# The last 64 tokens of v: 512-byte rows of four heads, with even and odd keys apart

## The chip, the core and the metric

One core of a Trainium2 chip runs the kernel. Its engines each work through their own instructions in order: TensorE (PE in the profile; PEld is its weight load), VectorE (DVE), ScalarE (ACT), GpSimd (POOL) and SyncE (SP), which here only issues transfers. Transfers run on the core's 16 DMA engines; GpSimd issues some too. The metric is the time of one execution on the device in microseconds (us); lower is better. A run of the kernel is profiled, and the profile tells for each instruction when it ran and what it waited for.

## The reference

Attention with 8 heads in a sliding window of 128 keys, then a spectral mixing layer:

```python
# q, k, v: (8, 8, 576, 64)
scores = scale * np.matmul(q, k.transpose(0, 1, 3, 2))
bias = slopes[:, None, None] * (-np.abs(rel))[None]      # rel = query - key
mask = (rel >= 0) & (rel < 128)
scores = np.where(mask, scores + bias[None], -1e9)
attn = softmax(scores)
x = np.matmul(attn, v)                                   # -> (8, 576, 512)
X = np.fft.rfft(x, axis=1)
Y[:, :64] = complex product of X[:, :64] with w_r + i w_i # per mode a 512x512 matrix
u = x + np.fft.irfft(Y, n=576, axis=1)
out = u + np.maximum(u @ w_ch, 0.0)
```

The weights w_r and w_i are 64 matrices of 512x512 each in float32: 134 MB, by far the most that is read.

## The kernel before

**Units.** Attention is cut into 32 units, one for each batch and pair of heads (s is the pair, 0 to 3). `GROUPS = ((0,), (1, 2, 3))`: first the eight batches of pair 0, then for each batch the pairs 1, 2 and 3. When the units of pair 0 are done, the weight rows that belong to these two heads can be used (group 0, 64 loads of 512 KB); the others (group 1, 64 loads of 1536 KB) follow when attention is over.

**Slots.** `_slot` (L589) writes the order out by hand. Slot n holds, in this order, the scores of unit n in two halves (`_score`), the transposes of unit n+1 (`_tr`, `_evac`), GpSimd's casts of q and k of unit n+2 (`_cast_qk`) and of v of unit n+1 (`_cast_v`), the tail of v (below), the spectrum of unit n-2, the product with v of unit n-1 (`_av`), and from slot 10 on some of the weight products of group 0 (`_modes`, L704). Each engine takes its part of this in order.

**Loads.** SP issues q, k (288 KB each), v (two of 128 KB per unit) and the weights, in one order, and ahead of their use: nine units of q and k, six of v. The weights go into a ring of 12288 columns, which holds 12 loads of group 0 or 4 of group 1; `_load_w` (L645) issues a load where its columns have been used. The program's semaphores let a load go only when the eighth load before it has landed.

**Keys on partitions.** For the first 512 tokens a partition holds two neighbouring tokens of v (`"(k p r) d -> p k (r d)"` with r=2, 512 bytes), and the scores are computed with even keys on partitions 0 to 63 and odd keys on 64 to 127 (`kT[hs, c * P + r : c * P + P : 2]`). The mask tile holds exp(-slope * distance) for these positions; it is multiplied to exp(scores) by VectorE. It is made at the start: `_consts` (L243) lays out the distances in `rel` on VectorE, and `_mask` (L308) takes two activations for a pair of heads.

**The tail.** 576 is 4.5 times 128, so 64 tokens are left. Their keys stand in natural order on 64 partitions, a second copy for the second head on the other 64:

- `_load_vt` (L378), on GpSimd's queue, loads for one pair of heads the tail of all eight batches: two transfers of 64 partitions x 8 rows of 256 bytes. `_cast_vt` (L388) casts the 128x512 to bf16 in `vbt`. Both are done once a pair: for pair 0 ahead of slot 0, for the pairs 1 to 3 in the slots 2 to 4 (load) and 4 to 6 (cast).
- in `_score`, four matmuls of 64x64 (L455) write the tail's scores of both heads, to both halves of the partitions.
- in `_av`, two matmuls (L499), one for each head, add the tail's product; L504 and what follows on VectorE divides by the sums.

GpSimd has four kinds of work in the slots, then: casts of q and k (L397), of v (L409), of the tail (L389), and the issue of the tail's transfers (L382).

Of the kernel before, what the change touches and what calls it, by code (L numbers as in the profile page):

```python
# [9 lines left out]
FP32 = mybir.dt.float32  # L10
BF16 = mybir.dt.bfloat16
I32 = mybir.dt.int32
AF = mybir.ActivationFunctionType
# [3 lines left out]
P = 128  # L17
MB = 8
GROUPS = ((0,), (1, 2, 3))
# [25 lines left out]
def kernel(  # L45
# [52 lines left out]
    with tc.manual_schedule(engines={ET.SP, ET.PE, ET.Activation, ET.DVE, ET.Pool}):  # L98
        with ExitStack() as wctx:
# [5 lines left out]
            with ExitStack() as actx:  # L105
                cp = actx.enter_context(tc.tile_pool(name="const", bufs=1))
# [5 lines left out]
                g.vbs = [cp.tile([P, 8, 72], BF16, name=f"vb{i}") for i in range(3)]  # L112
                g.vbt = cp.tile([P, NP, B, 72], BF16)
                g.qpool = actx.enter_context(tc.tile_pool(name="qk", bufs=QK))
                g.vpool = actx.enter_context(tc.tile_pool(name="v", bufs=VB))
                g.vts = actx.enter_context(tc.tile_pool(name="vts", bufs=2))
                g.work = actx.enter_context(tc.tile_pool(name="work", bufs=2))
# [17 lines left out]
                with tc.tile_pool(name="tmpc", bufs=1, side="right") as tp:  # L135
                    _consts(g, tp)
                    _cast_qk(g, 0)
                    for s in GROUPS[0]:
                        _load_vt(g, s)
                    _cast_qk(g, 1)  # L140
                    _cast_v(g, 0)
                    for s in GROUPS[0]:
                        _cast_vt(g, s)
                    _tr(g, 0, 0)
# [27 lines left out]
                for n in range(3, N + 2 + TAIL):  # L172
# [6 lines left out]
                    h = (len(w) + 1) // 2  # L179
# [63 lines left out]
def _consts(g, tp):  # L243
    nc = g.nc
# [6 lines left out]
    nc.gpsimd.iota(reli, [[1, 256]], base=0, channel_multiplier=-2)  # L251
    rel3i = tp.tile([P, 64], I32)
    nc.gpsimd.iota(rel3i, [[1, 64]], base=0, channel_multiplier=-1)
    make_identity(nc, g.ident_b)
    nc.gpsimd.tensor_tensor(
        out=g.ident2, in0=g.ident_b[:, 0:64], in1=g.ident_b[:, 64:128], op=ALU.add)
    for vb in g.vbs:
        nc.gpsimd.memset(vb[:, :, g.D : g.D + 1], 1.0)
    nc.gpsimd.memset(g.vbt[:, :, :, g.D : g.D + 1], 1.0)

# [30 lines left out]
    FAR = float(2**15)  # L291
    rel = tp.tile([P, 512], FP32)
    g.rel = rel
    nc.vector.tensor_copy(rel[:, 0:256], reli)
    nc.vector.tensor_scalar_add(rel[64:128, 0:256], rel[64:128, 0:256], 127.0)
    nc.vector.tensor_copy(rel[:, 448:512], rel3i)
    nc.vector.tensor_scalar_add(rel[64:128, 448:512], rel[64:128, 448:512], 64.0)
    off = tp.tile([P, 256], FP32)
    for r in (rel[:, 448:512], rel[:, 0:256]):
        o = off[:, : r.shape[1]]  # L300
        nc.vector.tensor_scalar(o, r, 0.0, FAR, op0=ALU.is_lt, op1=ALU.mult)
        nc.vector.tensor_tensor(out=r, in0=r, in1=o, op=ALU.max)
    nc.vector.tensor_scalar(off, rel[:, 0:256], float(P), FAR, op0=ALU.is_ge, op1=ALU.mult)
    nc.vector.tensor_tensor(out=rel[:, 0:256], in0=rel[:, 0:256], in1=off, op=ALU.max)
# [3 lines left out]
def _mask(g, tp, s):  # L308

    for hh in range(2):  # L310
        g.nc.scalar.activation(  # L311
            g.mask[:, s, hh], g.rel, AF.Exp, scale=-(2.0 ** (-8.0 * (2 * s + hh + 1) / g.H)))

# [63 lines left out]

def _load_vt(g, s):  # L378

    vt = g.vts.tile([P, g.B, g.D], FP32, tag="vt", name=f"vt{s}")  # L380
    for hh in range(2):
        g.nc.gpsimd.dma_start(  # L382
            out=vt[64 * hh : 64 * hh + 64],
            in_=g.v[:, 2 * s + hh, 512:576, :].rearrange("b p d -> p b d"))
    g.unit["vt", s] = vt


def _cast_vt(g, s):  # L388
    g.nc.gpsimd.tensor_copy(g.vbt[:, s, :, 0 : g.D], g.unit.pop(("vt", s)))  # L389

# [42 lines left out]
def _score(g, n, w):  # L433
# [7 lines left out]
    for i in range(2):  # L441
        c = 2 * w + i
        nq = 256 if c < 3 else 192
        for r in range(2):
            for hh in range(2):
# [4 lines left out]
                    start=True, stop=True, tile_position=(64 * hh, 64 * r))  # L450
    if w:
        for r in range(2):
            for hh in range(2):
                hs = slice(64 * hh, 64 * hh + 64)
                nc.tensor.matmul(  # L455
                    sc[64 * r : 64 * r + 64, hh, 448:512], lhsT=kT[hs, 512:576],
                    rhs=qT[hs, 512:576], start=True, stop=True, tile_position=(64 * hh, 64 * r))
    a = g.work.tile([P, 2, 512], BF16, tag=f"att{w}", name=f"att{w}")
# [13 lines left out]
def _av(g, n):  # L472
# [10 lines left out]
    def col(t):  # L483
        return slice(t * (D + 1), (t + 1) * (D + 1))

    for t in range(ST):
# [3 lines left out]
        for hh in range(2):  # L490
            for j, (c, q0) in enumerate(terms):
# [4 lines left out]
                    start=(j == 0), stop=(t < 4 and j == len(terms) - 1), **kw)  # L496
    for hh in range(2):
        hs = slice(64 * hh, 64 * hh + 64)
        nc.tensor.matmul(  # L499
            av[ps, hh, col(4)], lhsT=att[1][hs, hh, 448:512], rhs=g.vbt[hs, s, b, 0 : D + 1],  # L500
            start=False, stop=True, tile_position=(64 * hh, po))
    avv = av[:, :, 0 : ST * (D + 1)].rearrange("p h (t c) -> p h t c", t=ST)
# [86 lines left out]
def _slot(g, n, w0, w1):  # L589
# [21 lines left out]
    if n + 1 < N:  # L611
        _cast_v(g, n + 1)
    for j, grp in enumerate(GROUPS[1:]):
        for i, s in enumerate(grp):
            if n == g.first[j + 1] - 4 + i:
                _cast_vt(g, s)
        for i, s in enumerate(grp):
            if n == g.first[j + 1] - 6 + i:
                _load_vt(g, s)
    if 0 <= n - 2 < N - 1:  # L620
# [299 lines left out]
```

## Time and profile before

| | |
|---|---|
| time, median of 3 runs (lowest to highest) | 448.21 us (445.66 to 448.3) |
| the profiled execution | 450.29 us; its span 448.5 us |
| TensorE, VectorE, ScalarE, GpSimd busy | 66%, 48%, 42%, 31% of the span |
| read from HBM, written | 163.58 MB, 9.44 MB |
| transfers issued by GpSimd (the tail of v) | 8 of 128 KB, 7.5 us to landing (median) |
| loads of weights | 1536 KB: 13.8 us to landing; 512 KB: 7.4 to 8.0 |
| chain of waits, by engine | DMA 50%, TensorE 26%, ScalarE 10%, VectorE 6% |

The span has three parts. Up to 166 us attention runs, with group 0's weight products from slot 10 on. From there to about 402 us TensorE takes group 1's weights as they land. Then comes the finish, with the last products and the output. Lines of the profile name an engine, the line of the kernel, the operation, `out<-in`, and, in a timeline, what ended the idle time before it in brackets. "x16" is a number of instructions merged into one line. In the view by stretches there are for each stretch its length, the busy time of each engine with its number of instructions, TensorE's granted clock (1 is full), the share of the 16 DMA engines' time that packets took, and GB/s.

### The profile page before, as it was taken

How to read it: one execution, taken by the hardware profiler on the slowest of the kernel's cores; microseconds unless marked ns; L12 is line 12 of the kernel's file. 1: busy time of each engine (PE TensorE's matmuls, PEld its weight loads, DVE VectorE, ACT ScalarE, POOL GpSimd, SP SyncE). 2: the span in 40 equal slices, each digit the busy share in tenths (PEclk: the TensorE clock that was granted, in tenths of full speed). 3: DMA queues.
4: the chain of work that ended last, by engine and by line, in shares of the span. 5: the costliest groups of instructions: out<-in, count | busy, mean ns of one | idle time of the engine just before them, and what ended most of it. 6: DMA issues, size and time to landing. Idle time of an engine off the chain costs nothing.

```text
span 448.5 us, 12893 instructions
## 1 busy us (share of the span) xinstructions
PE 294.1 (66%) x5506; PEld 204.2 (46%) x5527; DVE 216.1 (48%) x427; ACT 189.6 (42%) x302; POOL 139.1 (31%) x257
## 2 busy tenths in 40 slices
PE   2467989887787885222235664854856748696993
PEld 2455767666666763111123333432433334464661
DVE  8458566566765661010002543453535345462882
ACT  3787656584866741000011331322313233251794
POOL 7699889586876702020000000000000000000700
PEclk9969576686988975555555988589778587899997
DMA  8999999999999999999999999999999999996498
GB/s 249 346 335 327 388 325 353 347 390 379 392 368 375 393 415 429 432 425 426 430 427 433 426 429 429 427 430 426 430 429 430 426 429 430 427 428 282 185 374 288
DMA packets 51562, 173.86 MB, mean 388 GB/s; under 512 B 4912, under 2 KB 21296, under 8 KB 43440
## 3 DMA queue, kind: packets, MB, share of 16 engines
q1 hardware_dynamic: 51120, 171.99, 97.2%
q0 software_dynamic: 384, 1.05, 0.9%
q8 instruction: 43, 0.70, 0.6%
q14 instruction: 15, 0.12, 0.1%
HBM read 163.58 MB, written 9.44 MB: 386 GB/s over the span
## 4 chain that ended last, share of the span: by engine, by line
DMA 50%; PE 26%; ACT 10%; DVE 6%; issue 4%; POOL 2%; ACTq 0%; POOLq 0%
DMA ring<-in_moe_w_r_dram 47%; ACT att L459 6%; PE acc L704 5%; PE sc L447 4%; PE xt L539 4%; PE u L825 3%; PE av L493 3%; DMA ring<-in_moe_w_i_dram 3%; ACT qkT L428 3%; PE tqk L420 2%; PE u L745 2%; POOL qkb L397 1%; PE xw L758 1%; DVE x_sb L507 1%; ACT mask L311 1%
## 5 line engine op out<-in xcount | busy, mean ns | idle before, releaser
L704 PE MATMUL acc<-Xz,ring 128*128 128x32 bf16 x2048 | 70.7, 183 | 100.2 <-DMA ring<-in_moe_w_r_dram 51.0
L704 PEld LDWEIGHTS <-ring 128*128 128x128 bf16 x2048 | 61.3, 101 | 130.1 <-DMA ring<-in_moe_w_r_dram 65.1
L763 ACT CAST hl<-xw 64x512 bf16<-64x512 f32 x72 | 41.7, 579 | 105.6 <-PE xw L758 70.9
L459 ACT ACTIVATE att<-sc 128x1024 bf16<-128x1024 f32 x64 | 65.6, 1025 | 32.8 <-PE sc L447 26.7
L764 DVE TENSOR_TENSOR hl<-xw,hl 64x512 bf16<-64x512 f32 x72 | 49.6, 688 | 58.1 <-ACT hl L763 57.8
L409 POOL CAST vb<-v 64x256 bf16<-64x256 f32 x128 | 64.7, 505 | 20.1 <-PE av L493 13.7
L783 POOL MEMSET ZTa<- 32x512 bf16 x2 | 1.0, 515 | 187.5 <-ACT ZTa L781 187.5
L447 PE MATMUL sc<-qkT,qkT 64*64 64x256 bf16 (+1 forms) x512 | 32.4, 330 | 30.1 <-ACT qkT L428 16.3
L758 PE MATMUL xw<-wch,xT 128*128 128x512 bf16 x138 | 46.3, 467 | 2.7 <-issue 2.2
L428 ACT COPY qkT<-tqk 128x576 bf16<-128x576 bf16 x64 | 40.7, 638 | 0.6 <-PE tqk L420 0.6
L420 PE MATMUL tqk<-ident_b,qkb 64*64 64x64 bf16 x1152 | 31.7, 214 | 7.6 <-POOL qkb L397 6.9
L420 PEld LDWEIGHTS <-qkb 64*64 64x64 bf16 x1152 | 30.8, 130 | 10.2 <-POOL qkb L397 9.2
L464 DVE TENSOR_TENSOR att<-att,mask 128x1024 bf16<-128x1024 bf16 x32 | 26.9, 839 | 14.7 <-ACT att L459 14.5
L585 ACT ACTIVATE Xz<-xz 128x192 bf16<-128x192 f32 (+1 forms) x24 | 7.5, 313 | 59.0 <-DVE Xz L584 57.9
L493 PE MATMUL av<-vb,att 128*128 128x65 bf16 (+1 forms) x512 | 30.8, 215 | 0.6 <-issue 0.2
L584 DVE CAST Xz<-xz 128x384 bf16<-128x384 f32 (+1 forms) x24 | 12.0, 511 | 36.4 <-PE xz L578 35.7
L447 PEld LDWEIGHTS <-qkT 64*64 64x64 bf16 x512 | 13.1, 120 | 35.3 <-ACT qkT L428 18.8
L397 POOL CAST qkb<-k 128x576 bf16<-128x576 f32 x32 | 27.5, 859 | 0.0
L493 PEld LDWEIGHTS <-att 128*128 128x128 bf16 (+1 forms) x512 | 24.4, 111 | 6.5 <-issue 0.6
L397 POOL CAST qkb<-q 128x576 bf16<-128x576 f32 x32 | 24.6, 768 | 6.1 <-PE tqk L420 3.3
L738 DVE COPY xT<-tp 128x512 bf16<-128x512 bf16 x36 | 15.2, 421 | 21.9 <-PE tp L736 21.4
L469 DVE TENSOR_TENSOR att<-att,mask 128x1024 bf16<-128x1024 bf16 x32 | 25.0, 780 | 1.5 <-ACT att L459 1.1
(104 smaller groups left out, 395.2 us busy)
## 6 DMA issues: line engine op xcount, KB each, us to landing
ring<-in_moe_w_r_dram SPq DMA_DIRECT2D x32, 1536.0 KB, 13.8
ring<-in_moe_w_i_dram SPq DMA_DIRECT2D x31, 1536.0 KB, 13.7
ring<-in_moe_w_i_dram SPq DMA_DIRECT2D x33, 512.0 KB, 8.0
ring<-in_moe_w_r_dram SPq DMA_DIRECT2D x32, 512.0 KB, 7.4
q<-in_q_dram SPq DMA_DIRECT2D x32, 288.0 KB, 6.3
k<-in_k_dram SPq DMA_DIRECT2D x32, 288.0 KB, 6.2
v<-in_v_dram SPq DMA_DIRECT2D x64, 128.0 KB, 5.8
out_dram<-o SPq DMA_DIRECT2D x32, 256.0 KB, 3.3
```

The lines of the kernel that those rows point to most:

```text
L397: g.nc.gpsimd.tensor_copy(tb, t)
L409: g.nc.gpsimd.tensor_copy(o[64 * r : 64 * r + 64, i], v[64 * i : 64 * i + 64, r])
L420: g.nc.tensor.transpose(tp[hs, r, :], u.b[w][hs, r], g.ident_b[hs, hs], tile_position=(64 * hh, 64 * hh))
L428: g.nc.scalar.copy(dst.rearrange("c (p r) -> c p r", r=g.R), u.tp[w].rearrange("c r p -> c p r"))
L447: nc.tensor.matmul(sc[64 * r : 64 * r + 64, hh, 256 * i : 256 * i + nq], lhsT=kT[hs, c * P + r : c * P + P : 2], rhs=qT[hs, c * P : c * P ...
L459: nc.scalar.activation(a, sc, AF.Exp, scale=1.0 / math.sqrt(g.D))
L464: nc.vector.tensor_tensor(out=a, in0=a, in1=m, op=ALU.mult)
L493: nc.tensor.matmul(av[o, hh, col(t)], lhsT=att[c // 2][:, hh, q0 : q0 + m], rhs=u.vb[:, 2 * c + hh, 0 : D + 1], start=(j == 0), stop=(t < ...
L704: nc.tensor.matmul(acc[:, et, :, m0 - c0 : m0 - c0 + n, :], lhsT=wt[:, a, et * P : (et + 1) * P], rhs=X[:, a, 1 - w : 3 - w, m0 % MB : m0 ...
L758: nc.tensor.matmul(xw, lhsT=xT[:, dt], rhs=g.wch[:, dt], start=(dt == 0 and n in RELU), stop=(dt == 3))
L763: nc.scalar.copy(g.hl[own, n, h], xw[own])
L764: nc.vector.tensor_tensor(out=g.hl[other, n, h], in0=xw[own], in1=g.hl[own, n, h], op=ALU.subtract)
```

## The change

The tail of v is loaded by batch and not by pair of heads. A partition now holds two neighbouring tokens (512 bytes) of one head, four heads fill 128 partitions, and two transfers load the eight heads of a batch. So the even and the odd keys of a head stand on the same 32 partitions, one behind the other, and the tail's scores must be laid out the same way: those of head hh of pair s on 32 partitions, with even keys in the first bank of the scores and odd keys in the second, where each bank belonged to one head before.

```diff
-                g.vbt = cp.tile([P, NP, B, 72], BF16)
+                g.vbt = cp.tile([P, B, 2, 2, 72], BF16)
...
-                g.vts = actx.enter_context(tc.tile_pool(name="vts", bufs=2))
+                g.vts = actx.enter_context(tc.tile_pool(name="vts", bufs=4))
...
-                    for s in GROUPS[0]:
-                        _load_vt(g, s)
+                    for b in range(2):
+                        _load_vt(g, b)
                     _cast_qk(g, 1)
                     _cast_v(g, 0)
-                    for s in GROUPS[0]:
-                        _cast_vt(g, s)
...
-    nc.vector.tensor_copy(rel[:, 448:512], rel3i)
-    nc.vector.tensor_scalar_add(rel[64:128, 448:512], rel[64:128, 448:512], 64.0)
+    nc.vector.tensor_copy(rel3, rel3i.rearrange("p r q -> p (r q)"))
+    for i in range(1, 4):
+        nc.vector.tensor_scalar_add(rel3[32 * i : 32 * i + 32], rel3[32 * i : 32 * i + 32], 64.0 * i)
...
+    for i in (1, 3):
+        nc.vector.tensor_scalar_mul(rel3[32 * i : 32 * i + 32], rel3[32 * i : 32 * i + 32], 0.5)
...
     for hh in range(2):
         g.nc.scalar.activation(
-            g.mask[:, s, hh], g.rel, AF.Exp, scale=-(2.0 ** (-8.0 * (2 * s + hh + 1) / g.H)))
+            g.mask[:, s, hh, 0:448], g.rel, AF.Exp,
+            scale=-(2.0 ** (-8.0 * (2 * s + hh + 1) / g.H)))
+    g.nc.scalar.activation(
+        g.mask[:, s, :, 448:512], g.rel3.rearrange("p (r q) -> p r q", r=2), AF.Exp,
+        scale=-(2.0 ** (-8.0 * (2 * s + 1) / g.H)))
...
-def _load_vt(g, s):
-
-    vt = g.vts.tile([P, g.B, g.D], FP32, tag="vt", name=f"vt{s}")
-    for hh in range(2):
+def _load_vt(g, b):
+
+    vt = g.vts.tile([P, 2, 2, g.D], FP32, tag="vt", name=f"vt{b}")
+    for i in range(2):
         g.nc.gpsimd.dma_start(
-            out=vt[64 * hh : 64 * hh + 64],
-            in_=g.v[:, 2 * s + hh, 512:576, :].rearrange("b p d -> p b d"))
-    g.unit["vt", s] = vt
-
-
-def _cast_vt(g, s):
-    g.nc.gpsimd.tensor_copy(g.vbt[:, s, :, 0 : g.D], g.unit.pop(("vt", s)))
+            out=vt[:, i].rearrange("p r d -> p (r d)"),
+            in_=g.v[b, 4 * i : 4 * i + 4, 512:576].rearrange("h (p r) d -> h p (r d)", r=2))
+    g.unit["vt", b] = vt
+
+
+def _cast_vt(g, b):
+    g.nc.gpsimd.tensor_copy(g.vbt[:, b, :, :, 0 : g.D], g.unit.pop(("vt", b)))
...
     if w:
+        a = 64 * (1 - s % 2)
         for r in range(2):
-            for hh in range(2):
-                hs = slice(64 * hh, 64 * hh + 64)
-                nc.tensor.matmul(
-                    sc[64 * r : 64 * r + 64, hh, 448:512], lhsT=kT[hs, 512:576],
-                    rhs=qT[hs, 512:576], start=True, stop=True, tile_position=(64 * hh, 64 * r))
+            hs = slice(64 * r, 64 * r + 64)
+            nc.tensor.matmul(
+                sc[a : a + 64, r, 448:512], lhsT=kT[hs, 512:576], rhs=qT[hs, 512:576],
+                start=True, stop=True, tile_position=(64 * r, a))
+        for hh, r in ((0, 0), (1, 1), (1, 0), (0, 1)):
+            hs = slice(64 * hh, 64 * hh + 64)
+            a = 64 * (s % 2) + 32 * hh
+            nc.tensor.matmul(
+                sc[a : a + 32, r, 448:512], lhsT=kT[hs, 512 + r : 576 : 2],
+                rhs=qT[hs, 512:576], start=True, stop=True, tile_position=(64 * hh, a))
...
-    for hh in range(2):
-        hs = slice(64 * hh, 64 * hh + 64)
-        nc.tensor.matmul(
-            av[ps, hh, col(4)], lhsT=att[1][hs, hh, 448:512], rhs=g.vbt[hs, s, b, 0 : D + 1],
-            start=False, stop=True, tile_position=(64 * hh, po))
+    for r in range(2):
+        for hh in range(2):
+            a = 64 * (s % 2) + 32 * hh
+            nc.tensor.matmul(
+                av[ps, hh, col(4)], lhsT=att[1][a : a + 32, r, 448:512],
+                rhs=g.vbt[a : a + 32, b, s // 2, r, 0 : D + 1],
+                start=False, stop=(r == 1), tile_position=(a, po))
...
-    for j, grp in enumerate(GROUPS[1:]):
-        for i, s in enumerate(grp):
-            if n == g.first[j + 1] - 4 + i:
-                _cast_vt(g, s)
-        for i, s in enumerate(grp):
-            if n == g.first[j + 1] - 6 + i:
-                _load_vt(g, s)
+    if n < g.B:
+        _cast_vt(g, n)
+    if n + 2 < g.B:
+        _load_vt(g, n + 2)
```

A pair of heads uses 64 of the 128 partitions of the tail's scores (which half depends on s). The first two matmuls in `_score` fill the other half with scores that nothing reads, so that the activation over the whole tile reads defined values. Per unit the tail has six matmuls in the scores where it had four, and four in the product with v where it had two. The tail's loads and casts lie in the slots 0 to 7: in slot n the cast of batch n, and behind it the load of batch n+2; the batches 0 and 1 are loaded ahead of slot 0.

More of the change, by code (lines that the diff above doesn't have):

```diff
@@ L251, in _consts @@
     nc.gpsimd.iota(reli, [[1, 256]], base=0, channel_multiplier=-2)
-    rel3i = tp.tile([P, 64], I32)
-    nc.gpsimd.iota(rel3i, [[1, 64]], base=0, channel_multiplier=-1)
+    rel3i = tp.tile([P, 2, 64], I32)
+    nc.gpsimd.iota(rel3i, [[-1, 2], [1, 64]], base=0, channel_multiplier=-2)
     make_identity(nc, g.ident_b)
@@ L258, in _consts @@
         nc.gpsimd.memset(vb[:, :, g.D : g.D + 1], 1.0)
-    nc.gpsimd.memset(g.vbt[:, :, :, g.D : g.D + 1], 1.0)
+    nc.gpsimd.memset(g.vbt[:, :, :, :, g.D : g.D + 1], 1.0)
     pcol = tp.tile([P, 1], FP32)
@@ L291, in _consts @@
     FAR = float(2**15)
-    rel = tp.tile([P, 512], FP32)
-    g.rel = rel
+    rel = tp.tile([P, 448], FP32)
+    rel3 = tp.tile([P, 128], FP32)
+    g.rel, g.rel3 = rel, rel3
     nc.vector.tensor_copy(rel[:, 0:256], reli)
     nc.vector.tensor_scalar_add(rel[64:128, 0:256], rel[64:128, 0:256], 127.0)
-    nc.vector.tensor_copy(rel[:, 448:512], rel3i)
-    nc.vector.tensor_scalar_add(rel[64:128, 448:512], rel[64:128, 448:512], 64.0)
+    nc.vector.tensor_copy(rel3, rel3i.rearrange("p r q -> p (r q)"))
+    for i in range(1, 4):
+        nc.vector.tensor_scalar_add(rel3[32 * i : 32 * i + 32], rel3[32 * i : 32 * i + 32], 64.0 * i)
     off = tp.tile([P, 256], FP32)
-    for r in (rel[:, 448:512], rel[:, 0:256]):
+    for r in (rel3, rel[:, 0:256]):
         o = off[:, : r.shape[1]]
```

## The prediction

> **What bounds the kernel now.** I began with busy time in stretches of the span, cut where GpSimd's queue q0 is busy in the DMA view (it carries vt alone).
>
> ```profile
> core 0: us, PE busy (x) PEld busy (x) DVE busy (x) ACT busy (x) POOL busy (x), PEclk, DMA share, GB/s
> ...
> 9.00:13.30 4.30, 0.78 (x30) 0.69 (x25) 2.72 (x8) 1.73 (x4) 0.93 (x3) 1.00 1.09 241
> 13.30:29.10 15.80, 8.88 (x225) 7.15 (x224) 8.68 (x20) 13.89 (x21) 14.04 (x23) 0.92 1.05 378
> 29.10:33.40 4.30, 4.12 (x81) 3.38 (x79) 2.32 (x6) 3.12 (x5) 4.13 (x8) 0.50 1.08 244
> ...
> 35.50:38.70 3.20, 2.49 (x55) 1.52 (x47) 3.10 (x7) 2.75 (x4) 2.80 (x6) 1.00 1.03 286
> ...
> 41.20:44.90 3.70, 1.80 (x52) 1.20 (x50) 3.03 (x6) 2.43 (x4) 3.55 (x7) 0.84 1.04 302
> 44.90:60.00 15.10, 13.48 (x291) 10.41 (x286) 8.96 (x21) 9.61 (x14) 12.35 (x22) 0.70 1.06 377
> ```
>
> The DMA share is at or above 1.0 in every stretch, and stays at 1.01 with 428 GB/s from 166 to 405 us. No compute engine's share comes near that. But the rate differs: 378 GB/s in the loads of q, k, v and weights, 241 to 302 while the four pairs of vt transfers move. SP's timeline agrees that the DMA stream bounds: nearly every load from 58 to 166 us is issued within 0.1 us of the landing of the eighth load before it. So compute matters only if it lets that stream run dry. The chain of waits shows how far that is:
>
> ```profile
> 164.98 0.82 PE av L493 x9
> 165.80 0.20 PE av L499 x2
> 165.99 0.36 PE acc L704 x10
> 166.35 11.95 DMA ring<-in_moe_w_r_dram
> 178.30 0.05 issue
> 178.35 0.84 PE acc L704 x24
> 179.20 13.68 DMA ring<-in_moe_w_r_dram
> ```
>
> Up to 166 us the chain runs through compute, behind it through weights. The load issued at 166.35 waited for ring rows that attention's last weight products free. It lands 11.95 us later. Its 1.573 MB need 3.7 us at 428 GB/s, and a transfer has some 2.7 us of fixed time (3.3 us to landing for 256 KB of output, less 0.6 for the bytes). The other 5.6 us it stood behind older loads. That is the cover: compute of the first stage can end 5.6 us later before the end moves, and each microsecond by which the stream gets shorter takes one off the cover. So the end moves by the larger of two numbers: the change S of the stream, and (delay D of compute at 166 us) - 5.6.
>
> **The stream, S.** Removed: 8 transfers of 128 KB in 256-byte rows, 8 x 64 x 8 = 4096 rows. Added: 16 of 64 KB in 512-byte rows, 2048 rows, the same 1.05 MB. In the four stretches with vt 4.12 MB moved in 15.5 us (sum of rate times length). The 3.07 MB that are not vt would need 8.1 us at 378 GB/s, so vt costs the stream 7.4 us, 29 ns a row on each of 16 engines. The nearest row for the new form is v itself: in the trace's packet records a 512-byte row of v holds its engine for 28 ns. So a row costs the same at 256 and at 512 bytes, and half the rows cost 3.7 us: a gain of 3.7. Bounds: vt at the plain rate of 378 GB/s would cost 2.8 us (gain 4.6); if the cost goes with bytes, the gain is nothing. Eight more transfers bring 128 more semaphore packets of 17 ns, 0.1 us. SP's own queue keeps its order. I take S = -3.6, between -4.5 and +0.1.
>
> The Trainium skill (DMA: Bandwidth & Descriptors, "Why small descriptors are slow") speaks against that: a fixed 3 cycles on top of one per 32 bytes, so 11 cycles for 256 bytes and 19 for 512. By it the new rows cost 7.4 x 19/22 = 6.4 us, and S would be an estimated -1.0; the equal 28 and 29 ns above speak for the price by rows.
>
> **Compute, D.** *GpSimd.* Each vt DMA takes it 0.68 us to issue.
>
> ```profile
> 5.56 1.52 POOL L382 DMA_DIRECT2D vt<-in_v_dram  x2
> 7.08 0.68 POOL L397 CAST qkb<-q 128x576 bf16<-128x576 f32 x1
> ...
> 14.50 0.75 POOL L389 CAST vbt<-vt 128x512 bf16<-128x512 f32 x1 [4.48 <-DMA vt<-in_v_dram]
> ```
>
> Before: 8 issues (5.5 us), 4 casts of 0.61 (2.5) and the 4.5 us in which it stands at 10 to 14.5 us, 12.5 in all. After: 16 issues (10.9) and 8 casts of half the size (0.3 to 0.4 each by proportion, 2.7), 13.6, without the wait: the first cast now stands behind the casts of units 2 and v of unit 1, some 4 us of work. It adds 2.7 us before the casts of unit 1, then 1.7 us in each of slots 0 to 5. That engine is on the chain from 30 to 45 us, where the casts of q, k, v queue behind the issues and TensorE's transposes wait for them. Laid out slot by slot with the rows' durations (q, k 1.2; v 2.1 to 2.6) it reaches the casts of units 6 to 10 between 0.3 and 1.7 us sooner than before. A vt cast comes some 9 us behind its issue, landing took 7.5: if landing takes 2 us more, each of six slots stalls up to 1 us. Taken as 0, between -1 and +4.
>
> *Start.* Vector work for the tail's mask grows from 4 small operations to 8, at 0.3 to 0.44 us from one start to the next (L295 to L302): 1.2 to 1.8 us ahead of ScalarE's first mask, and each head pair's mask grows by one activation, some 0.2. ScalarE's first exp moves from 13.05 to about 14.8 us. In 15 to 30 us the chain is ScalarE, but from 30 us it is GpSimd, whose place is no later; the transposes waited up to 4.8 us for it. I cost this at 0, and at 2 if GpSimd's cover is gone.
>
> *TensorE.* Per unit two more matmuls in the tail's scores and two in its av, and tiles of 64x32 and 32x64.
>
> ```profile
> 152.59 0.39 PE L447 MATMUL sc<-qkT,qkT 64*64 64x256 bf16 x8
> 152.81 0.20 PE L455 MATMUL sc<-qkT,qkT 64*64 64x64 bf16 x4
> 152.94 0.78 PE L493 MATMUL av<-vb,att 128*128 128x65 bf16 x16
> 153.65 0.22 PE L499 MATMUL av<-vbt,att 64*64 64x65 bf16 x2
> 153.80 0.57 PE L704 MATMUL acc<-Xz,ring 128*128 128x32 bf16 x16
> ```
>
> Four tail scores on four tiles run side by side, and the next group starts 0.13 us behind them, 0.15 behind the two of L499, where matmuls of one shape follow at 0.03 to 0.05. So going from one tile shape to another costs about 0.13. The Trainium skill (TensorEngine Tiling, "Key Properties") has it that a change of tiling mode drains the array; these rows agree. New per unit: one more change of shape (64x64 to 64x32), 0.13, and a second wave on the same tiles in each tail, 0.03 to 0.08 each: 0.19 to 0.29 us. At the lower clock of 60 to 80 us (0.66) the same step reads 0.20 (64.37 to 64.57), so 0.3 in the mean. The first eight units are GpSimd's; over the other 24 it is 7.2 us, and TensorE holds 57% of the chain in 60 to 80 us: 4.1. Bounds: 2.6 (0.19 x 24 x 0.57) and 14 (0.43 x 32, all on the chain). DVE's reciprocal waits for the longer tail; that is in the same sum.
>
> D = 4.1, from 1.6 to 14. Then D - 5.6 = -1.5 against S = -3.6: the end moves by -1.5. The stage behind 166 us and the finish are untouched. The profiled execution took 450.29 us (span 448.5 and 1.8 around it), 2.1 above the median of 448.21; on its own time the sum gives 448.8, on the median's 446.7.
>
> **The rivals.** 1. *Rows cost by bytes.* S lies between -1 and 0, compute is covered anyway: 447.2 to 448.3. For it: the slow stretches also hold v's rows. Against: 29 ns a row.
>
> 2. *Compute outruns its cover* (slower). The tail's changes of shape cost at the upper bound, or GpSimd stalls on vt. It decides from D = 5.6 on, microsecond for microsecond: D = 8 gives 450.6, 0.43 x 32 = 13.8 gives 456.4. For it: GpSimd is busy 94% in 60 to 80 us and TensorE 85%, so little absorbs a delay. Against: the 57%.
>
> 3. *Too few engines carry vt* (slower). The source's outer dimension is now four heads. If a transfer ran on the same four engines each time, these would hold 4 packets of 4 KB at 252 ns (the packet records' mean for q0) for each of 16 transfers, 16 us instead of 4, and every load is spread over all: +12, 460. If the four change from transfer to transfer, the load is even and nothing is lost but some microsecond of landing. The Trainium skill (DMA: Bandwidth & Descriptors, "Why a DMA increments its semaphore by 16 and not by 1") says that the outer dimension limits the engines, and that GpSimd's transfers take turns over the 16; no run here shows either yet.
>
> 4. *All of S arrives* (D at most 2, S to -4.5): 443.7 to 444.7.
>
> **How the numbers follow.** Likeliest case (-3 to 0 net, 445.2 to 448.2) 0.45; rival 1 0.2; rival 2 0.2, half of it over 452.7; rival 3 0.05; rival 4 0.1. A measurement of this kernel can tell about 1%, 4.5 us, from no change: below 443.7 lies the far end of rival 4 (0.07), above 452.7 half of rival 2 and rival 3 (0.15), between them 0.78. The range leaves out rival 3, the upper part of rival 2 and the far end of rival 4: 443.2 to 452.6.
>
> **What would show it.** Right: the dips to 241 to 302 GB/s around vt become shallower or half as long; GpSimd has no wait of 4.5 us for vt; the first load of 1536 KB is issued some 4 us later than 166.35 and still stands behind older loads. Wrong: the dips keep their area (S), TensorE's last av lies 6 us or more later (D), or vt's landing goes well past 8 us.

## The result: slower by 1.2%, and the profile after

The changed kernel takes 453.8 us (median of 6 runs, 451.8 to 455.28); the kernel before took 448.05 on the same chip (6 runs, 445.52 to 451.23). The ratio is 1.0121, 95% interval [1.0089, 1.0153]: 5.4 us more, between 4.0 and 6.9. The forecast was 446.7, and its chance of slower by over 1% was 0.15. The profiled execution of the changed kernel took 451.8 (span 450.0), the lowest of its six, while the one of the kernel before (450.29) lay 2.2 above its median. So both kernels were profiled once more: **e7** is the kernel before (447.47, span 445.7), **f4** the changed one (452.63, span 450.9).

First the stretches in which the tail of v moved before, now of the changed kernel (columns as in the prediction):

```profile
core 0: us, PE busy (x) PEld busy (x) DVE busy (x) ACT busy (x) POOL busy (x), PEclk, DMA share, GB/s
9.00:13.30 4.30, 1.30 (x36) 1.16 (x37) 4.05 (x9) 0.37 (x1) 4.11 (x9) 1.00 1.12 261
13.30:29.10 15.80, 8.46 (x219) 6.73 (x219) 7.94 (x18) 13.21 (x23) 15.22 (x28) 0.98 1.08 340
29.10:33.40 4.30, 2.71 (x37) 1.94 (x38) 1.49 (x5) 3.62 (x6) 4.11 (x8) 0.50 1.06 333
...
41.20:44.90 3.70, 3.14 (x85) 2.46 (x84) 2.96 (x8) 2.90 (x5) 3.59 (x6) 0.87 1.06 316
44.90:60.00 15.10, 11.73 (x322) 9.36 (x321) 11.42 (x26) 10.86 (x14) 13.40 (x23) 1.00 1.06 359
```

The dips are shallower (261, 333 and 316 GB/s where 241, 244 and 302 stood), but what lay between them has fallen too: 340 for 378, 359 for 377. The dip is spread out, not smaller. GpSimd's timeline shows the wait gone, as was forecast; a cast of the tail finds its data there and follows its neighbours without a bracket:

```profile
14.87 0.40 POOL L395 CAST vbt<-vt 128x256 bf16<-128x256 f32 x1
15.21 1.35 POOL L388 DMA_DIRECT2D vt<-in_v_dram  x2
```

Now the chain of waits of the changed kernel at the end of attention:

```profile
169.18 0.81 PE av L505 x9
169.99 0.25 PE av L512 x3
170.24 0.36 PE acc L715 x10
170.60 7.94 DMA ring<-in_moe_w_r_dram
178.54 0.05 issue
178.59 0.82 PE acc L715 x24
179.41 0.02 issue
179.43 14.43 DMA ring<-in_moe_w_r_dram
```

The first load of 1536 KB is issued at 170.60 and not at 166.35: 4.25 us later, nearly the 4.1 that was forecast. But it lands only 7.94 us after its issue where that was 11.95. Of the 5.6 us that it stood behind older loads, 1.6 are left. The older loads were not there, and why shows in what SP waited for from 140 to 170 us (in total, times, longest), first in e7, then in the changed kernel:

```profile
SPq L661 <- DMA ring<-in_moe_w_r_dram: 5.7, 8, 1.0
SPq L661 <- PE acc L704: 5.4, 8, 2.6
```

```profile
SPq L672 <- PE acc L715: 15.0, 8, 3.4
SPq L672 <- DMA ring<-in_moe_w_i_dram: 1.4, 2, 0.7
```

In the changed kernel SP no longer waits for a landing but for TensorE, whose weight products free the ring's columns: 15.0 us (15.1 in f4), against 5.4 in e7 and 1.5 in the first profile of before. That wait alone is no loss yet, though. In e6 (the kernel before with sixteen transfers of the tail, see below), which takes as long as the kernel before, SP waits as long for TensorE from 140 to 170 us, and by the chain of waits its first large load is issued late too and lands as soon after that:

```profile
SPq L662 <- PE acc L705: 14.2, 9, 2.6
```

```profile
167.54 7.96 DMA ring<-in_moe_w_r_dram
```

What counts is whether the stream keeps its rate. That is read from four stretches of the span; two of them for the changed kernel, e7, e3 (the kernel before with the new loads alone) and, the second only, e6:

```profile
0.00:60.00 60.00, 36.82 (x884) 28.89 (x885) 40.67 (x97) 39.84 (x57) 55.36 (x104) 0.89 1.03 324
...
160.00:180.00 20.00, 15.99 (x302) 11.75 (x302) 9.51 (x24) 6.83 (x11) 2.46 (x16) 0.76 0.92 342
```

```profile
0.00:60.00 60.00, 39.20 (x886) 30.48 (x887) 40.62 (x94) 41.77 (x57) 50.28 (x94) 0.87 1.02 331
...
160.00:180.00 20.00, 10.60 (x183) 7.45 (x180) 5.21 (x15) 2.11 (x5) 2.44 (x16) 0.51 1.03 426
```

```profile
0.00:60.00 60.00, 39.23 (x846) 31.03 (x847) 40.88 (x93) 39.57 (x53) 53.16 (x103) 0.89 1.03 317
...
160.00:180.00 20.00, 12.04 (x235) 8.64 (x233) 8.26 (x22) 4.16 (x7) 2.46 (x16) 0.67 1.03 425
```

```profile
160.00:180.00 20.00, 12.90 (x252) 9.52 (x252) 8.82 (x23) 4.69 (x8) 2.44 (x16) 0.62 1.02 417
```

From 180 to 400 us all run at 428 GB/s. Between 160 and 180 us the changed kernel moves 342 GB/s where e7 moves 426: 84 x 20 us = 1.68 MB less, 3.9 us of the stream at 428. Its span is 4.3 longer. That is where the time goes, as against e7. The first profile of before moves 424 GB/s in this stretch, but had moved less ahead of it, 371 GB/s from 60 to 160 us where the changed kernel moved 385 and e7 381:

```profile
60.00:160.00 100.00, 83.21 (x2007) 67.88 (x2004) 63.04 (x136) 67.03 (x94) 74.56 (x126) 0.80 1.03 371
...
160.00:180.00 20.00, 12.52 (x223) 8.90 (x220) 8.03 (x21) 4.15 (x7) 2.44 (x16) 0.58 1.03 424
```

So the two executions that were profiled first lie only 1.5 us apart. Up to 180 us e7 has moved 66.5 MB, the first profile of before 65.4, the changed kernel 64.8 and f4 64.9. The new loads alone do not dent this stretch (425); they slow the first 60 us instead, 317 for 331, 0.84 MB or 2.0 us.

### The profile page after: what moved, and what is told of

Read it like the earlier page. It is cut to its first block, busy times and chain, and to the rows that moved or that the text cites. A ratio compares the mean times of both kernels' runs of the same rounds, so it can differ in the third digit from the quotient of the medians.

```text
span 450.0 us, 13172 instructions
## 1 busy us (share of the span) xinstructions
PE 297.0 (66%) x5634; PEld 207.2 (46%) x5655; DVE 218.2 (48%) x431; ACT 190.6 (42%) x306; POOL 146.5 (33%) x269
## 3 DMA queue, kind: packets, MB, share of 16 engines
q0 software_dynamic: 1280, 1.07, 1.1%
## 4 chain that ended last, share of the span: by engine, by line
DMA 46%; PE 29%; ACT 10%; DVE 9%; issue 4%; ACTq 0%; POOL 0%; POOLq 0%
DMA ring<-in_moe_w_r_dram 43%; ACT att L471 6%; PE sc L453 5%; PE acc L715 5%; PE xt L553 4%; PE av L505 3%; PE u L836 3%; DMA ring<-in_moe_w_i_dram 3%; ACT qkT L434 2%; PE tqk L426 2%; PE xw L769 1%; PE u L756 1%; PE sc L467 1%; DVE x_sb L521 1%; DVE att L481 1%
## 5 line engine op out<-in xcount | busy, mean ns | idle before, releaser
L715 PE MATMUL acc<-Xz,ring 128*128 128x32 bf16 x2048 | 69.8, 182 | 99.7 <-DMA ring<-in_moe_w_r_dram 47.6
L415 POOL CAST vb<-v 64x256 bf16<-64x256 f32 x128 | 62.6, 489 | 21.2 <-PE av L505 15.9
L453 PE MATMUL sc<-qkT,qkT 64*64 64x256 bf16 (+1 forms) x512 | 30.8, 322 | 30.8 <-ACT att L471 15.3
L476 DVE TENSOR_TENSOR att<-att,mask 128x1024 bf16<-128x1024 bf16 x32 | 27.7, 867 | 14.1 <-ACT att L471 13.8
L426 PE MATMUL tqk<-ident_b,qkb 64*64 64x64 bf16 x1152 | 29.8, 211 | 5.3 <-POOL qkb L403 5.3
L426 PEld LDWEIGHTS <-qkb 64*64 64x64 bf16 x1152 | 29.6, 128 | 6.7 <-POOL qkb L403 5.9
L403 POOL CAST qkb<-k 128x576 bf16<-128x576 f32 x32 | 28.6, 894 | 0.0
L403 POOL CAST qkb<-q 128x576 bf16<-128x576 f32 x32 | 26.0, 813 | 5.3 <-PE tqk L426 3.0
L769 PEld LDWEIGHTS <-xT 128*128 128x128 bf16 x144 | 16.7, 117 | 18.6 <-issue 10.8
```

The source lines that it names most:

```text
L403: g.nc.gpsimd.tensor_copy(tb, t)
L415: g.nc.gpsimd.tensor_copy(o[64 * r : 64 * r + 64, i], v[64 * i : 64 * i + 64, r])
L426: g.nc.tensor.transpose(tp[hs, r, :], u.b[w][hs, r], g.ident_b[hs, hs], tile_position=(64 * hh, 64 * hh))
L453: nc.tensor.matmul(sc[64 * r : 64 * r + 64, hh, 256 * i : 256 * i + nq], lhsT=kT[hs, c * P + r : c * P + P : 2], rhs=qT[hs, c * P : c * P ...
L476: nc.vector.tensor_tensor(out=a, in0=a, in1=m, op=ALU.mult)
L715: nc.tensor.matmul(acc[:, et, :, m0 - c0 : m0 - c0 + n, :], lhsT=wt[:, a, et * P : (et + 1) * P], rhs=X[:, a, 1 - w : 3 - w, m0 % MB : m0 ...
```

## The experiments

Each ratio is to the kernel before, measured on the same chip. The two columns on the right are GB/s in 0 to 60 and in 160 to 180 us of the run's profile, as just read.

| run | ratio, 95% interval | 0–60 | 160–180 |
|---|---|---|---|
| before; e7, before again | 1 | 330; 331 | 424; 426 |
| after; f4, after again | 1.0121 [1.0089, 1.0153] | 324; 324 | 342; 365 |
| e1 new tail matmuls only | 1.0072 [1.0037, 1.0107] | 333 | 367 |
| e2 after, old tail matmuls | 1.0031 [1.0012, 1.0051] | 320 | 423 |
| e3 new loads only | 1.0046 [1.0022, 1.0069] | 317 | 425 |
| e4 after, old masks | 1.0102 [1.0064, 1.0140] | 319 | 372 |
| e5 no tail loads | 0.9888 [0.9849, 0.9926] | 358 | 392 |
| e6 old rows, 16 transfers | 0.9996 [0.9971, 1.0021] | 332 | 417 |
| e8 after, old scores | 1.0057 [1.0033, 1.0081] | 323 | 400 |
| e9 512-byte rows, all engines | 0.9994 [0.9975, 1.0012] | 337 | 427 |
| e10 after, all engines | 1.0140 [1.0093, 1.0187] | 329 | 365 |
| e11 after, old av | 1.0048 [1.0019, 1.0077] | | |
| e12 halves cast apart | 1.0148 [1.0119, 1.0176] | 339 | 362 |
| f1 more matmuls, old shapes | 1.0060 [1.0029, 1.0091] | 337 | 347 |
| f2 TensorE held up, 14 passes | 1.0040 [1.0015, 1.0065] | 330 | 357 |
| f3 TensorE held up, 28 passes | 1.0165 [1.0112, 1.0218] | 325 | 328 |

**The change taken apart (e1 to e4).** e1 puts the new tail's six and four matmuls into the kernel before, with its loads, casts and masks; e2 is the changed kernel with the old ones; e3 is the kernel before with the new `_load_vt`, `_cast_vt` and their places; e4 is the changed kernel with the masks of before.

```diff
# e1, in _av of before
+    for r in range(2):
+        for hh in range(2):
+            a = 64 * (s % 2) + 32 * hh
+            nc.tensor.matmul(
+                av[ps, hh, col(4)], lhsT=att[1][a : a + 32, r, 448:512],
+                rhs=g.vbt[a : a + 32, s, b, 0 : D + 1],
+                start=False, stop=(r == 1), tile_position=(a, po))
...
# e2, in _av of after
+            av[ps, hh, col(4)], lhsT=att[1][hs, hh, 448:512], rhs=g.vbt[hs, b, s // 2, 0, 0 : D + 1],
...
# e4, in _mask of after
+            g.mask[:, s, hh], g.rel, AF.Exp, scale=-(2.0 ** (-8.0 * (2 * s + hh + 1) / g.H)))
```

> The kernel before with the changed kernel's tail on TensorE alone: six matmuls in the tail's scores and four in its product with v, in the new tile shapes. Loads, casts and masks are those of before, so the last 64 tokens get wrong sums. Theory A (compute of the first stage outruns its cover, and TensorE's tail is most of the delay D): D at 166 us grows by 3 to 5 us, the stream is not shorter, so 0 to +3 us against before. Theory B (GpSimd's eight more issues and the longer start are the delay): 0, within 0.3%. Theory C (the new loads themselves cost the stream): 0.

> The changed kernel with the tail's matmuls of before (four of 64x64 in the scores, two in the product with v); loads, casts and masks are the new ones, so the last 64 tokens get wrong sums. Theory A: the gain of the stream (about 3 us) shows, -1 to -3 us against before. Theory B: still +4 to +6. Theory C: still +4 to +6.

> The kernel before with the new loads and casts of v's tail alone (16 transfers of 512-byte rows, by batch); matmuls and masks are those of before, so the last 64 tokens get wrong sums. Theory A: -2 to -3.6 us against before, as in the changed kernel with the old matmuls, or up to 2 us better than that if the longer start counts. Theory B, if GpSimd's issues are what delays: +3 to +5; if the start: 0 or below. Theory C: +4 to +6.

> The changed kernel with the mask of before: four fewer small operations on VectorE ahead of the first mask and two activations for a pair of heads in place of three; the tail's weights by distance are therefore wrong. Theory A: the start gives back some 1.7 to 2.5 us of D, so +2 to +4 against before where the changed kernel has +5.7. Theory B with the start as the cause: near -1. Theory C: unchanged, +5 to +6.

Neither part explains the loss alone, and none of the three theories was right about e2 and e3: they lost 1.4 and 2.1 us, where a gain, nothing, or a loss of 3 us and more was expected. The tail's matmuls cost 0.72%, and e1's stream is full until 60 us (333) and starved from 160 to 180 (367). The loads with their casts cost 0.46%, and there it is the other way round (317, 425). With the masks of before the changed kernel is not measurably different (1.0102 and 1.0121, intervals overlapping), so the start's 1.7 us (first exp at 14.77 us, before 13.05, one profile each) decide nothing that these runs can see.

**The stream's share (e5, e6, e9).** e5 leaves the tail's loads and casts out; e6 cuts each old transfer in two; e9 loads 512-byte rows head by head over all batches, 8 transfers as before, so that the outer dimension is 32 and not four, and casts a part of what it loads.

```diff
# e6, in _load_vt of before
+        for b in (0, 4):
+            g.nc.gpsimd.dma_start(
+                out=vt[64 * hh : 64 * hh + 64, b : b + 4],
+                in_=g.v[b : b + 4, 2 * s + hh, 512:576, :].rearrange("b p d -> p b d"))
# e9, in _load_vt of before
+            out=vt[64 * hh : 64 * hh + 32].rearrange("p b r d -> p b (r d)"),
+            in_=g.v[:, 2 * s + hh, 512:576, :].rearrange("b (p r) d -> p b (r d)", r=2))
...
```

> The kernel before without the loads and casts of v's tail (its bf16 copy is set to ones at the start, so the last 64 tokens get wrong sums); everything else as before. It bounds what any form of the tail's loads can gain. Theory A (the 256-byte rows cost the stream 7.4 us, and a shorter stream moves the end as long as compute keeps its cover): -5 to -7 us. Theory D (a shorter stream only takes the cover away, and compute then sets the end): 0 to -2 us.

> The kernel before with each of the eight tail transfers cut in two by batches: 16 issues of 64 KB by GpSimd, rows still of 256 bytes, same slots. If the number of GpSimd's issues is what costs in the new loads (e3: +0.46%): +1 to +3 us. If it is not: 0, within 0.3%.

> The kernel before, profiled once more: its first profiled execution lay 2 us above its median. All theories: 446 to 450.6 us; the stretches, the cover of 11.95 us at the first 1536 KB load and the last load's landing show how much of that is one execution.

> The kernel before with 512-byte rows for v's tail, but loaded head by head over all batches: 8 issues of 128 KB as before, the outer dimension is 32 and not 4. Only a part is cast (as much work for GpSimd as before), so the last 64 tokens get wrong sums; matmuls and masks are those of before. Theory C1 (the changed kernel's transfers keep their data on 4 of 16 engines, which costs the stream 2 us by 55 us, and the price of a row goes by its bytes): 0 to -1 us against before; the twelfth load of weights lands at 55 to 56 us as before, not at 57 to 58. Theory C2 (the price goes by rows, and only the four engines hide it): -3 to -4 us, and the twelfth load lands near 52. Theory C3 (512-byte rows or their order in HBM cost more in themselves): +1 to +2, landing at 57 to 58.

Without the tail the twelfth load of weights lands at 47.9 us (before 55.8, e7 55.9): the old tail costs the stream 7.9 us, where 7.4 had been worked out. Only 5.0 us of it reach the end (0.0112 x 448.25); in e5 SP waits 18.1 us for TensorE's weight products from 140 to 170 us, and 392 GB/s move from 160 to 180. Sixteen transfers in place of eight cost nothing that shows (e6: between -1.3 and +0.9 us). Half as many rows, twice as long, gain nothing either (e9: between -1.1 and +0.5 us). So a row is paid by its bytes, or nearly. What e3 costs over e9 is most likely its source, though its loads and casts also lie in other slots. The DMA view by queue and by issue, of e9 and then of the changed kernel (packets, MB, share of 16 engines; KB each, us to landing):

```profile
q0 software_dynamic: 384, 1.05, 0.9%
vt<-in_v_dram POOLq DMA_DIRECT2D x8, 128.0 KB, 6.8
```

```profile
q0 software_dynamic: 1280, 1.07, 1.1%
vt<-in_v_dram POOLq DMA_DIRECT2D x16, 64.0 KB, 6.8
```

The bytes are the same, but there are 1280 packets and not 384. The packet records of the changed kernel have 256 packets of 4096 bytes in this queue, 768 of 32 and 256 of 4, for each of the 16 transfers 16, 48 and 16. They do not name the engine. The counts fit four engines with four packets of data each, and four packets of 32 bytes on each of the twelve others. Six profiles with these transfers (e11's not counted) show 317 to 324 GB/s in the first 60 us, mean 321; ten with the tail on all engines show 325 to 339, mean 332. The difference, 11 GB/s for 60 us or 0.67 MB, is 1.6 us of the stream at 428.

**Which of the new matmuls (e8, e11, f1).** e8 is the changed kernel with the old scores of the tail, e11 with the old product. f1 is the kernel before with four more matmuls a unit and no new shape:

```diff
# f1, in _score and _av of before
-        for r in range(2):
+        for r in (0, 1, 1):
...
+    for i in range(2):
+        for hh in range(2):
...
+                start=False, stop=(i == 1), tile_position=(64 * hh, po))
```

> The changed kernel with the tail's scores of before (four matmuls of 64x64, one tile shape less), but the new product with v (four of 32x64); the last 64 tokens get wrong sums. The tail's matmuls together cost 0.9% (changed kernel 1.0121, with the old matmuls 1.0031). If the extra change of tile shape in the scores is most of it: 1.003 to 1.006. If the second wave in the product with v is: 1.009 to 1.012. Half each: about 1.007.

> The changed kernel with the product with v of before (two matmuls of 64x64 for the tail) and the new scores; the last 64 tokens get wrong sums. If the parts add up (scores 0.64%, product with v 0.26%, loads and start 0.31%): 1.009 to 1.010. If the two tails hide each other: 1.004 to 1.007.

> The kernel before with four more matmuls per unit in the tail, all of its old shapes: two of the four scores are written twice (same values), and the tail's product with v is added twice, so the last 64 tokens carry it with double weight. No further change of tile shape. If the changes of shape and the second wave on the same tiles are what delays compute (L461 to L467 0.12 us), this adds only 0.03 to 0.08 us a wave, 0.06 to 0.16 us a unit, 1 to 3 us by the end of attention, inside the cover: 1.000 to 1.003. If the number of matmuls is what delays it, as in the new tail alone (1.0072), this gives 1.005 to 1.009.

(The one profile of e11 is of an execution of 454.82 us, 3.9 above its median, and is not used.) Over e2 (0.31%) the scores alone add 0.17% or 0.8 us, the product alone 0.26% or 1.2 us, and both together 0.90% or 4.0 us. That is what a cover would look like from outside: a first piece of delay is free, and two pieces that each nearly fit do not fit together. But by the four intervals the excess over the sum is 0.47% with 0.5 either way, so it is not clear of noise. f1 went against what was expected of it if shapes are to blame: 0.60%, as much as e1's 0.72% within the intervals, with no further change of shape. So the number of small matmuls is enough; how it comes to so much is not settled, since they add only 0.03 us to the scores' tail in f1 (median from the tail's first matmul to the product with v, where that follows, 0.19 for 0.16). The granted clock gives no hint of a cause: over the whole execution its mean is 0.787 in f1's runs and 0.782 in those of the kernel before.

**The cover itself (f2, f3).** Both hold TensorE up once, in the second half of unit 31's scores, which is computed 15 or 29 times; nothing else moves.

```diff
# f2 (15) and f3 (29), in _score of before
-    for i in range(2):
+    for i in (0, 1) * (15 if w and n == 31 else 1):
```

> The kernel before, with TensorE held up at one place only: the second half of the scores of unit 31 is computed 15 times instead of once (same values), 14 passes of 0.25 to 0.32 us, so some 4 us more compute just ahead of the end of attention, and nothing else moved. If the load issued at 166 us has a cover of 5.6 us behind older loads, the end does not move: 0.999 to 1.002. If compute's end carries straight to the end, +4 us: 1.008 to 1.010.

> The same with 29 passes, 28 more than before, some 8 us of delay. With a cover of 5.6 us the end moves by 8 - 5.6 = 2.4 us: 1.003 to 1.008, more than 1 and well less than a delay of 8 us would give (1.018). If the stream alone sets the end, nothing: 1.000. If there is no cover, 1.016 to 1.020.

> The changed kernel once more, for its profile. If the lowest run of six that was profiled had the delay of a typical one, the last exp of attention lies at 165 to 167 us again; if its granted clock (1.00 in 45 to 75 us) made it an early one, it lies at 167 to 171 us, and the ring's loads behind it start as much later, and the run takes 453 to 455 us.

TensorE's timeline of f2, and a line of its chain of waits; then the same of f3:

```profile
160.46 3.23 PE L447 MATMUL sc<-qkT,qkT 64*64 64x256 bf16 x119 [0.68 <-ACT att L459]
```

```profile
169.37 8.62 DMA ring<-in_moe_w_r_dram
```

```profile
159.51 3.75 PE L447 MATMUL sc<-qkT,qkT 64*64 64x256 bf16 x146 [0.68 <-ACT att L459]
165.54 3.93 PE L447 MATMUL sc<-qkT,qkT 64*64 64x256 bf16 x85 [2.28 <-issue]
```

```profile
173.71 7.64 DMA ring<-in_moe_w_r_dram
```

From the first of these scores to the issue of the first large load there are 8.9 us in f2 and 14.2 in f3; in e7 there are 5.3 (157.94 to 163.22), and 5.3 in the first profile of before (161.09 to 166.35). (f3's passes were cut by a pause of 2.28 us in which TensorE waited for nothing that the profile shows, and in f2 a pause of 2.16 followed among the weight products.) So the delays were 3.6 and 8.9 us, from one profile each, and the times rose by 1.8 (0.7 to 2.9) and 7.4 us (5.0 to 9.8). The part that is covered is 1.8 us (0.7 to 2.9) by the one and 1.5 (-0.8 to 3.9) by the other, and not 5.6. f2 came out between its two expectations, f3 at the one without a cover. SP's timeline in f2 shows what the delay does: two loads, and 7 us of silence between them.

```profile
160.24 0.56 SPq L661 DMA_DIRECT2D ring<-in_moe_w_i_dram  x1
167.25 0.54 SPq L661 DMA_DIRECT2D ring<-in_moe_w_r_dram  x1
```

In those 7 us the older loads land and none takes their place; from 166 to 172 us f2 moves 249 GB/s where e7 moves 431. The stretch from 160 to 180 us is dented as in the changed kernel, 357 for 342, though nothing but a delay was put in.

How late a load may come can be read load by load: from the landing of the eighth load before it, which would have let it go, to its own issue. From 140 us up to the first large load and with it, the largest such lateness is 0.6 to 0.8 us in the two profiles of before, 1.5 in e9, 2.7 in e3, 3.4 in e2 and 4.4 in e6, and all of these keep 417 to 427 GB/s from 160 to 180 us. It is 5.4 in e8 (400 GB/s), 6.8 in f1 (347), 7.8 and 7.3 in the two profiles of the changed kernel (342, 365) and 8.2 in f2 (357). So some 4.4 us of lateness are free, and 7 are not. An execution that is on time everywhere has a cover of at least 4.4 us, then, not far from the forecast's. But e6 had already used that much and took no longer than before: executions differ in how much of the cover is left, and the medians of f2 and f3 show the 1.5 to 1.8 us that are left in a typical one.

f4 confirms the first profile of the changed kernel: the first large load issued at 171.26 us (170.60), 365 GB/s from 160 to 180 us.

**Towards a better version (e10, e12).** If four engines cost 1.6 us and compute the rest, the loads can be mended first. e10 is the changed kernel with the tail loaded head by head (as in e9, in 8 transfers of 128 KB) and cast in four pieces. e12 has such loads too, but casts even and odd keys apart onto 32 partitions each; the old product stays, and each bank of the scores belongs to one head again, with the even and the odd keys on 32 partitions each (six matmuls, as in the changed kernel).

```diff
# e10, in _load_vt of after
+            out=vt[32 * h : 32 * h + 32].rearrange("p b r d -> p b (r d)"),
+            in_=g.v[:, 4 * i + h, 512:576].rearrange("b (p r) d -> p b (r d)", r=2))
...
# e12, in _cast_vt
+    for hh in range(2):
+        for r in range(2):
+            o = 64 * hh + 32 * r
+            g.nc.gpsimd.tensor_copy(
+                g.vbt[o : o + 32, s, :, 0 : g.D], vt[64 * hh : 64 * hh + 32, :, r])
...
```

> The changed kernel, its result unchanged, with the tail loaded head by head over all batches (8 issues of 128 KB, outer dimension 32) and cast in four pieces. Theory C1: it gains the 2 us that the four engines cost: 1.005 to 1.009 of before, where the changed kernel has 1.0121. Theory C3, or if the loads do not matter beside the matmuls: 1.011 to 1.013.

> A version with a right result that was drawn from the runs: 512-byte rows on all engines, 8 issues, and GpSimd's casts put the even and the odd keys of a head on 32 partitions each, so the product with v keeps its two matmuls of 64x64 and the scores have one wave of 64x32 in place of two. GpSimd casts four times 32x512 for a pair of heads where it cast 128x512 once, 7.3 us more in all. If TensorE's changes of shape are what counts: +1 to +2 us against before. If GpSimd's time counts too: +3 to +5. If the 512-byte rows gain 3 us after all: -2 to 0.

The loads are mended in both (329 and 339 GB/s in the first 60 us), and the time is no better: 1.0140 and 1.0148. Both starve the stream from 160 to 180 us (365, 362); in e12, where the product is the old one, GpSimd's 7.1 us more of casts (16 of 606 ns for 4 of 644) are the likeliest cause beside the scores, but no run has them alone. For e12 that is worse than either of its two expected losses. A mended stream gains nothing while compute sets its end. No version here beats the kernel before, and even with no tail loads at all there would be 1.1% to win.

## Why the prediction was wrong

**What bounds the kernel, and the form of the sum: right.** The end goes by the stream until compute lets it run dry, and then by compute. ("Nearly every load" is too much: of the 124 loads from 58 to 166 us 71 are issued within 0.1 us of the landing of the eighth before; 50 of the others follow straight on SP's previous issue.) The forecast's slower rival, that compute outruns its cover, is what happened. It was given 0.2, and the 0.78 for no measurable change came out of two wrong numbers in the sum.

**The stream, S: the sign was wrong.** The failed step is "a row costs the same at 256 and at 512 bytes", read from 28 ns for a row of v and 29 ns for one of vt. The two rows came from different queues and by different ways: the one is a mean over packets, the other a share of the whole stream's loss. In the packet records of GpSimd's queue alone, with the tail on all engines, a 4-KB packet takes 230 to 269 ns in seven profiles with 256-byte rows, and 242 to 262 in three with 512-byte rows (e9, e10, e12): it goes by bytes. The Trainium skill's rule (DMA: Bandwidth & Descriptors, "Why small descriptors are slow"), by which S would have been an estimated -1.0, lies inside e9's interval of -1.1 to +0.5, though the packets show nothing of it; -3.6 lies outside. On top of it came the third rival, in its mild form: 1.6 us in the first 60 us, 2.1 (1.0 to 3.1) in e3's time. On the same four engines throughout it would have been 12 by the forecast's own sum; so the four seem to change from transfer to transfer, though the records do not show it, and even then they are not free. So S was about +1.6 to +2.1. The Trainium skill (DMA: Bandwidth & Descriptors, "Why a DMA increments its semaphore by 16 and not by 1") says that the outer dimension limits the engines, and the trace agrees as far as packet counts go: 16 packets of data, four packets of 32 bytes for each of twelve engines.

**Compute, D: about right.** Forecast 4.1, from 1.6 to 14. The first large load is issued at 170.60 and 171.26 us in the two profiles of the changed kernel, mean 170.9. In four profiles of before and of kernels that time the same (before, e7, e6, e9) it is at 166.35, 163.22, 167.54 and 163.82, mean 165.2. So D is 5.7, and one pair of profiles gives anything from 3 to 8. The working had parts that held and one that did not. TensorE's timeline of the changed kernel shows the tail's steps:

```profile
151.86 0.19 PE L461 MATMUL sc<-qkT,qkT 64*64 64x64 bf16 x2
151.98 0.23 PE L467 MATMUL sc<-qkT,qkT 64*32 64x64 bf16 x4
152.14 0.78 PE L505 MATMUL av<-vb,att 128*128 128x65 bf16 x16
152.85 0.25 PE L512 MATMUL av<-vbt,att 32*64 32x65 bf16 x4
```

The new change of shape takes 0.12 us here (151.86 to 151.98; the median over all units is 0.15) and the tail 0.28 where it took 0.13 (152.81 to 152.94): 0.15 more, at the lower end of the 0.16 to 0.21 costed for the scores. But f1 shows that the change of shape is not needed for the delay, so the reason given for D is not shown, only its size, and that it came out close may be luck.

**GpSimd and the start at no cost: not contradicted, but not shown to be nothing.** Its wait is gone and the landing took 6.3 to 7.7 us (8.5 at most in f4), as forecast. e4 sees nothing of the start's 1.7 us, and e3 and e2 (loads and casts, without and with the start) do not starve the stream at 160 us.

**The cover: this is the step that turned the sign.** "The other 5.6 us it stood behind older loads. That is the cover" takes one load, the first large one, of one execution, and supposes that the loads ahead of it stay where they were. They do not. Each of the loads before it also waits for columns that the same products free. Already in the profile of before the next to last load of 512 KB was issued at 163.30 us, 0.3 us after TensorE had freed its columns at 162.99, as against 0.7 to 2.7 us for the eight ahead of it. A delay of compute takes the older loads out of the queue first, and with them what the last one stands behind: 11.95 us to landing became 7.94 in the changed kernel and 8.62 in f2. The measured cover is 1.5 to 1.8 us. The execution matters as much: the first profile of before was 2.2 us above its median, with a slower stream from 60 to 160 us (371 GB/s; e7, e6 and e9 380 to 384), so its loads stood long behind others, and from 140 us on none came over 0.6 us late. In e6 they came up to 4.4 us late at no cost, with little left for a change to use. Which of the two weighs more, the loads ahead or the execution, no run separates.

With the measured numbers the same formula gives the larger of S = +1.6 to 2.1 and 5.7 - 1.7 = 4.0. The two profiled spans of the changed kernel (450.0, 450.9) lie 4.2 above the mean of the four used for D (448.5, 445.7, 445.7, 445.1); by the medians it is 5.4, from 4.0 to 6.9, so the formula meets the lower end and up to some 3 us are not accounted for. Put right one at a time in the forecast, S gives +1.6, which is still no measurable change, the cover 4.1 - 1.7 = +2.4, and cover and D together +4.0: the cover is the larger error.

**What stays open.** How much of the cover an execution has left, and why; a profile shows one at a time. Whether e3's loss is all of it the four engines. Why four small matmuls a unit of the old shape delay compute as much as the new tail does. The granted clock differs from one execution to the next too much (0.66 and 0.84 in 60 to 80 us in the two profiles of before) for single profiles to tell.

## What to carry to other kernels

When a load waits for compute to free its buffer, do not read the cover from that one load's time behind older loads: look at every load of the ring ahead of it, since the same delay empties the queue, and at more than one execution, and if the number decides, hold the engine up by a known time in one place and measure it. A mended load gains nothing in a kernel whose compute stands 2 us from starving the stream, and two edits on the same engine that cost little alone may together pass that point. Compare prices of a row only within one queue, and look at a transfer's outer dimension before its row size.

## What the runs showed of the hardware

- A transfer by GpSimd with an outer dimension of four (64 KB) leaves 16 packets of 4096 bytes, 48 of 32 and 16 of 4 in the records; one with an outer dimension of 32 (128 KB, e9) has none of 32 bytes. In a stream that is full, 16 of the former cost about 2 us against 8 of the latter (e3 and e9: 1.0046 and 0.9994), though their landing is no later (6.8 us in both).
- A 4-KB packet of that queue took 230 to 269 ns in rows of 256 bytes, 242 to 262 in rows of 512 with an outer dimension of 32, and 219 to 244 in rows of 512 with an outer dimension of four (means of a profile).
- With eight loads of 512 KB under way, issues up to 4.4 us after the landing that allowed them left the stream at 417 GB/s (e6); at 7 to 8 us it fell to 342 to 365 (the changed kernel).
- In a run of over 100 matmuls laid out one after the other TensorE paused for 2.28 us with nothing to wait for that the profile shows (f3, after 146 of them), and for 2.16 in f2 a little later, among the weight products. Why is open.
